# Loading the first chunk's alpha, k and q by batch instead of by pairs of batches, in a new instruction order

## The chip, the core and the metric

The kernel runs on one core of one Trainium2 chip. The core has five engines, each with its own queue of instructions that it executes in order: PE (TensorE, matrix products; its weight loads, PEld, overlap them), DVE (VectorE), ACT (ScalarE), POOL (GpSimd) and SP (SyncE, which in this kernel only issues transfers). Transfers (DMAs) run on 16 DMA engines beside them. A tile is a piece of the on-chip memory; a semaphore tells an engine that what it needs is ready. The metric is the device time of one execution in microseconds (us).

## What is computed

First a gated linear recurrence, for 4 batches of 8 heads with 768 tokens and 48 numbers per head. Then, with the heads side by side in rows of 384, a two-layer network with a norm before it and the rows added back behind it.

```python
def _attn_ref(q, k, v, alpha) -> np.ndarray:
    B, H, S, D = q.shape                      # 4, 8, 768, 48
    state = np.zeros((B, H, D, D), dtype=np.float32)
    y = np.zeros_like(q)
    for t in range(S):
        state = alpha[:, :, t, :, None] * state + np.einsum('bhd,bhe->bhde', k[:, :, t], v[:, :, t])
        y[:, :, t] = np.einsum('bhd,bhde->bhe', q[:, :, t], state)
    return y.astype(np.float32)

def _moe_ref(x, g_ln, w_ch1, w_ch2) -> np.ndarray:   # w_ch1 384 x 1536, w_ch2 1536 x 384
    mu = np.mean(x, axis=-1, keepdims=True)
    var = np.mean((x - mu) ** 2, axis=-1, keepdims=True)
    xn = (x - mu) / np.sqrt(var + 1e-06) * g_ln
    ch = np.maximum(xn @ w_ch1, 0.0) @ w_ch2
    return (x + ch).astype(np.float32)
```

The two weight matrices arrive as float64 and are rounded to float32 on the chip. q, k, v and alpha are float32 and lie in memory token by token, all heads of a token side by side.

## The kernel before

**Tiling.** The 768 tokens are cut into 6 chunks of 128. For each chunk c and batch b there is one unit of attention, 24 in all. Within a chunk the recurrence is written as matrix products. ACT takes the logarithm of alpha (L308), PE sums the logarithms over the tokens (L313), ACT takes the exponential of the sums and of their negatives (L320, L321), and DVE multiplies them with k (L323) and q (L325). PE transposes both products (L351), which are copied out of PE's accumulators by ACT and DVE (L356, L358). PE multiplies them to scores (chunk 0: L393), DVE keeps the causal part of these (L407, a predicated copy), and PE multiplies k with v to the chunk's contribution to the state (L428) and the scores, and the state before, with v and q to the output (L454 for chunk 0, L459 and L463 for the later ones).

**The gate.** A batch's new state is scaled by its decay over the chunk, which is the last row of the exponentials. This row has to become columns, so it goes through memory: SP sends the row out right behind the product with q (L330), and later fetches it back as columns (L419, the tile `gate`). In chunk 0 the DVE instruction that needs the gate is L437; later chunks add on DVE (L441) and scale on POOL (L443).

**The network.** The output of a batch is normed (L504 to L511) and transposed (L522). The first layer of chunk 0 is L558 (all four batches in two groups), its second layer L570. The network of chunks 1 to 5 is done later by a scheme that trades products for sums: combinations of weights and rows on DVE, ACT and POOL, then products (L848 for the first layer, L674 for the second), and sums of these into the result (L661, L684, L687, L690).

**Weights.** There are 12 pieces. Each is loaded as float64 words by SP (L203) and rounded by DVE and ACT (L215 to L232). The L558 of chunk 0 needs the first pieces.

**Loads.** `load(c, m, names)` loads what `names` lists of chunk c for the pair m of batches (2m and 2m+1): one transfer of 384 KB each for alpha, k and q, and v (L141). Chunk 0's alpha is the exception, loaded by batch (192 KB). All input loads, rows, gates and weights go through SP's one queue, in the order in which the program issues them.

**The order.** The program is written as generators, one for each unit of work, and each `yield` ends a step. The string ORDER holds one letter for each step: the step's instructions are put on the engines' queues when its letter comes. So ORDER decides what each engine does in which order, and nothing is reordered afterwards.

- `a` to `x`: the attention of unit n (a is chunk 0's batch 0, b its batch 1, e chunk 1's batch 0)
- `A` to `L`: load and rounding of a piece of weights
- `Y`, `Z`, `P`, `Q`: first and second layer of chunk 0
- `S`, `W`, `X`, `N`: combinations of weights and rows; `1`, `2`, `R`, `U`: hidden products and what follows them; `M`: products of the second layer; `O`: fetches rows kept in memory

```python
    with tc.manual_schedule():
        for turn in ORDER:
            next(turns[turn], None)
```

**At the start** the four alpha loads of chunk 0 are issued by the program before the ORDER loop begins. In the attention of chunk 0 the even batch (b = 0 and b = 2) has two steps ahead of its logarithm: one that loads k and q of its pair of batches, and one that loads v of the pair. The odd batch has none. After its row has been sent out (L330), the step that follows in the odd batch of chunks 0 and 1 loads alpha, k and q of the next chunk for the pair. In the trace batch 1's row of chunk 0 is sent out after batch 0's.

Of the kernel before, what the change touches and what calls it, by code (L numbers as in the profile page):

```python
# [11 lines left out]
FP32 = mybir.dt.float32  # L12
# [18 lines left out]


ORDER = (
    "bacabcadaacbcaadbcadabcababbebaccbadbaaBbccaedcbceAeeaaacbfecfBcdafddeaedbdeafae"
    "bcdccbfgadhAdcgCcdbebeebfhggdfgbfffbCdcgfgecdfchgdfhgabcddchdhAiiegjhacehedhhjfg"
    "biAdfidAeBhBijffYYiCjZZYYifZYlZCgjYDlYYjjZZYBZYgDieEgDgDjZZekEhZYGZgZigZGeeYgYgg"
    "fZYEhfGfkChihiYFYijfgEhgkhFZYhgYfghijgkFeZZlGZShfZYHlhHfYFYZeZHelYiZgllPmZkJIgJk"
    "PeiYjJIflHeSZIQgkIlYSjiPkffennSQlOKjLSnSjmSQhKnSjLnKPkiljnhSQnLkkjkWknkShOmPhkhl"
    "kOOhWlmmphmQmkmXjWQnXjlSQjPmkilXSXkP2OXWjXQjkjW2iXoSWX2oWX22Pi2mnol1j1mom2omSpoo"
    "l1XSpk2oW2m112p1m2pm11m1W211pp12O122r22jnn21lpnmnjSml1riOn2l12Rl111kqS1m21W1Rkp2"  # L40
    "o21mUXpq1mU2rUrnmj1rl2Rno2oomqonrormpokO1rNM2Mipin1op1ionoqUM2qp2W12RkMmNqiMoRtk"
    "UrpkqNM1NoMliMlNUMMNMNMKNqMlNorMWrnmtltNRMsqppMWNMriMMMpNlsqqqnoqttNttMtMsXMMssM"
    "sMNMNMX1oXXppMvstM2MXMMNMsppXoMXoqMsMMXM1nqqv11Xq1trMq2tqX21rn12v1r2ur2r222rvsqs"
    "svsu1rs1nuvvt2s11ss11p22rtsvosn2uropuXru222221uts212stnU1211u1121222Op1Rp2tRU21R"
    "Us1pXqU11x2tO2MM1vwMUM12xuRvu1vurNNNNwtOuuMwRxvNtxRNutwwMM2MOwNXwMNuXMMtNM1rMMMw"
    "qtXMMMxNUNxtMMsNMMMxXxMtXtrMMqMNrMXNvutMMwNuMMMNMMMxMLMOM11vvuq2X2O2wMus1wX11222"
    "2r2Xt1222w22utsqxvw2x2ww1vx21sX12121xwvq2O2x2w111u1uvU121w12s1wuRvx12U11J1q21R1U"
    "OvRxU121wMMu2xxsRNMw2NNMRM1MUNN2MMuUMqXN1MrNNRMNvMXNXMMMM2MMMxNM1uNXMMNMNMOXMXMv"
    "MMXOMMMXxNxwxMMvNMMMMMXMx21w1x222212v12w222x122w2212X11UX2212121121121wx111MU11X"
    "2RR2v1211212211R1URU211XOUM2XNRX1MX1RM2MXN2MXNXNMXXMXMMMN111U1MN1M1122MNM1MM2MM1"  # L50
    "11NNN121O11NM1MM21N1112N1122M1MMM12MM12N222M22M2RM1M2N22MM2MU1ON2M22M2UURR22RNNM"
    "MNM1MMOMRMNMUUM2ONMNNNMO2MMMUMNMMMMMRMMNNMMMNMNMMNMMMMMMMMNMNMMMMMMM"
)


# [1 line left out]
def kernel(  # L57
# [36 lines left out]
    nc = tc.nc  # L94

    B, S, H, D = q.shape
    DM = H * D
    DF = w_ch1.shape[1]
    P = 128
    NCB = S // P  # L100
    NP = H // 2
# [7 lines left out]
    raw = ctx.enter_context(tc.tile_pool(name="raw", bufs=B // 2))  # L109
# [10 lines left out]
    r = np.arange(P)  # L120
# [3 lines left out]
    raws = {}  # L124

    def load(c, m, names):

        bs = range(2 * m, 2 * m + 2)
        rows = slice(c * P, (c + 1) * P)
        for n, src in (("a", alpha), ("k", k), ("q", q)):  # L130
            if n in names:
                t = raw.tile([P, 2, 2, NP, D], FP32, name=f"r{n}", tag="in", bufs=7)
                step = 1 if n == "a" and c == 0 else 2
                for i in range(0, 2, step):
                    nc.sync.dma_start(
                        t[:, i:i + step].rearrange("t b i p d -> t b (i p d)"),
                        src[bs.start + i:bs.start + i + step, rows].rearrange("b t h d -> t b (h d)"))
                raws.update({(n, c, b): t[:, b - bs.start] for b in bs})
        if "v" in names:
            vn = raw.tile([P, 2, 2, NP, D], FP32, name="vn", tag="vn")  # L140
            nc.sync.dma_start(vn.rearrange("t b i p d -> t b (i p d)"),  # L141
                              v[bs.start:bs.stop, rows].rearrange("b t h d -> t b (h d)"))
            vx = None
            if c:


                vx = raw.tile([P, 2, NP, D], FP32, name="vx", tag="vx")
                src = v[bs.start:bs.stop, rows].rearrange("b (s t) h d -> s t b (h d)", s=2)
                parts = ((0, 0, NP, NP), (1, 0, NP, 0))
                if c >= SPLIT:  # L150
                    parts = ((0, 0, NP, NP - 1), (1, 0, NP - 1, 0), (1, NP - 1, 1, H - 1))
                for h, to, n, at in parts:
                    nc.sync.dma_start(
                        vx[halves[h]].rearrange("t b p d -> t b (p d)")[:, :, to * D:(to + n) * D],
                        src[1 - h, :, :, at * D:(at + n) * D])
            for b in bs:
                raws["v", c, b] = vn[:, b - bs.start], vx[:, b - bs.start] if c else None

    lone = {}

    def load_one(n):
# [11 lines left out]
    nc.scalar.dma_start(consts, nc.inline_tensor(const_np, name="consts").ap())  # L173
    tri, ident = consts[:, :P], consts[:, P:2 * P]
    mask, mask_of_halves = tri.bitcast(INT32), consts[:, 2 * P:].bitcast(INT32)
    for m in range(B // 2):
        load(0, m, "a")

    w1 = cpool.tile([P, NJ // 2, NF, 2 * P], FP32, name="w1")
    w2 = cpool.tile([P, NJ, DM], FP32, name="w2")  # L180
# [113 lines left out]
    def attention(c, b):  # L294


        whole, last = c == 0, c + 1 == NCB
        split = c >= SPLIT
        if whole and b % 2 == 0:
            load(0, b // 2, "kq")  # L300
            yield
            load(0, b // 2, "v")
            yield

        qk = qk_of(c, b).rearrange("t n p i c -> t n i p c")[:, :, :, :, :D]
        eq = eq_of(c, b).rearrange("t p i c -> t i p c")[:, :, :, :D]
# [143 lines left out]
        for p in range(NP):  # L450
            for i in range(2):
                for s in range(2):
# [5 lines left out]
                    r = i if split and p == NP - 1 else 1 - i  # L458
# [11 lines left out]
        if split:  # L470


            xv, m = x.rearrange("t (i p d) -> t i p d", i=2, d=D), NP - 1
# [446 lines left out]
    turns = {"YZ"[h]: first_of_chunk_0(h) for h in range(2)}  # L920
    turns |= {"PQ"[h]: second_of_chunk_0(h) for h in range(2)}
    turns |= {chr(ord("a") + n): attention(n // B, n % B) for n in range(NCB * B)}
    turns |= {chr(ord("A") + i): take_weights(i) for i in range(len(pieces))}
    turns |= {"M": mlp(), "S": combine_first(), "W": combine_weights(),
# [35 lines left out]
```

## Time and profile before

| | |
|---|---|
| median of 3 runs | 421.02 us |
| lowest and highest | 420.24 and 422.59 us |
| the profiled execution | 420.14 us |
| its span, first to last instruction | 418.3 us |
| PE busy | 409.8 us (98%), 4608 matmuls |
| DVE busy | 351.4 us (84%), 713 instructions |
| ACT busy | 177.5 us (42%), 440 |
| POOL busy | 151.6 us (36%), 164 |
| moved by DMA | 61.26 MB, 146 GB/s on the mean |

Busy times are those of one profiled execution, as shares of its span. An engine counts as busy while it executes an instruction; PE's matmuls overlap each other, so its busy time is no sum of pure work. The view by stage gives the same for stretches of the span. The chain of waits starts at the last instruction and goes back, at each step to what released it, so that it names the work that set the end. "issue" in it is time in which the engine waited for nothing that the profile shows, and "st L441" the tile and line of an instruction. Queue waits are those of SP: "SPq L419" is the place in SP's queue of the gate's transfer, with the time at which it was issued and how long the queue stood there. A landing is the time at which a transfer's last byte has arrived.

### The profile page before, as it was taken

To read this page: it belongs to the slowest core of one execution; us is meant where nothing else is said; L and a number is where in the kernel's file an instruction comes from. 1 tells how busy PE (TensorE), PEld (TensorE's weight loads), DVE (VectorE), ACT (ScalarE), POOL (GpSimd) and SP (SyncE) were. 2 spreads that over 40 slices of the span, in tenths; PEclk is the share of its full clock that TensorE was granted. 3 is DMA by queue.
4 is the path that set the end of the run, shared out by engine and by line. 5 is a ranking of instruction groups with operands and counts; after the bars stand their busy time and mean duration, and the time that the engine had idled before them with its cause. 6 is when DMAs were issued, how large, how long until landed. Compare 5 with 4: busy or idle time off the path is not lost.

```text
span 418.3 us, 11560 instructions
## 1 busy us (share of the span) xinstructions
PE 409.8 (98%) x4608; PEld 361.3 (86%) x4608; DVE 351.4 (84%) x713; ACT 177.5 (42%) x440; POOL 151.6 (36%) x164
## 2 busy tenths in 40 slices
PE   7998999999999999999999999999999999999996
PEld 5787888766578889998889999889998899999996
DVE  4999999999999989996888995688876767977873
ACT  5598447724243496414546603364313242014110
POOL 1011000003203980043395033493152940499123
PEclk9999999999999999999999999999999999999999
DMA  8999999987888778587684546433035200001201
GB/s 278 340 302 288 235 196 306 270 184 195 193 233 175 207 153 193 123 203 179 135 213 85 130 102 162 88 96 78 0 116 102 67 0 2 1 19 40 94 20 56
DMA packets 135037, 61.26 MB, mean 146 GB/s; under 512 B 90908, under 2 KB 131100, under 8 KB 134984
## 3 DMA queue, kind: packets, MB, share of 16 engines
q1 hardware_dynamic: 134440, 60.37, 56.1%
q8 instruction: 36, 0.59, 0.6%
q10 hardware_dynamic: 544, 0.17, 0.2%
q14 instruction: 17, 0.14, 0.1%
HBM read 43.12 MB, written 17.39 MB: 145 GB/s over the span
## 4 chain that ended last, share of the span: by engine, by line
PE 89%; DVE 4%; DMA 2%; ACT 2%; issue 1%; POOL 0%; POOLq 0%; SPq 0%; DVEq 0%
PE hps L848 31%; PE ops L674 30%; PE ops L570 8%; PE hps L558 7%; PE aps L401 3%; PE yps L459 2%; PE yps L463 2%; PE sums L428 2%; DMA vn<-in_v_dram 2%; PE xps L522 1%; PE aps L393 1%; DMA ra<-in_alpha_dram 1%; PE lps L313 1%; DVE w L217 1%; PE tps L351 1%
## 5 line engine op out<-in xcount | busy, mean ns | idle before, releaser
L690 POOL TENSOR_TENSOR ob<-ob,u 128x192 f32<-128x192 f32 x40 | 26.2, 665 | 64.5 <-DVE ob L687 48.3
L848 PE MATMUL hps<-sum,w 128*128 128x256 f32 x192 | 46.3, 381 | 0.0
L898 ACT ACTIVATE hT<-hT 128x512 f32<-128x512 f32 x48 | 28.7, 622 | 35.0 <-POOL hT L870 18.5
L443 POOL TENSOR_TENSOR mid<-mid,gate 112x192 f32<-112x192 f32 x20 | 11.6, 580 | 81.8 <-DVE mid L441 51.3
L674 PE MATMUL ops<-w,hT 128*128 128x192 f32 x224 | 40.5, 327 | 0.0
L848 PEld LDWEIGHTS hps<-sum,w 128*128 128x128 f32 x192 | 36.1, 190 | 5.0
L674 PEld LDWEIGHTS ops<-w,hT 128*128 128x128 f32 x224 | 37.1, 190 | 0.7 <-issue 0.2
L848 PE MATMUL hps<-xT,w 128*128 128x256 f32 x136 | 34.0, 380 | 0.0
L570 PE MATMUL ops<-w,hT 128*128 128x384 f32 x96 | 33.0, 492 | 0.0
L558 PE MATMUL hps<-xT,w 128*128 128x256 f32 x144 | 32.5, 382 | 0.0
L558 PEld LDWEIGHTS hps<-xT,w 128*128 128x128 f32 x144 | 27.0, 190 | 4.2
L674 PE MATMUL ops<-ws,sum 128*128 128x192 f32 x160 | 28.7, 327 | 0.0
L848 PEld LDWEIGHTS hps<-xT,w 128*128 128x128 f32 x136 | 25.5, 190 | 3.1
L570 PEld LDWEIGHTS ops<-w,hT 128*128 128x128 f32 x96 | 17.5, 190 | 10.8 <-DVE w L232 0.4
L674 PEld LDWEIGHTS ops<-ws,sum 128*128 128x128 f32 x160 | 26.5, 190 | 0.3
L684 DVE TENSOR_TENSOR ob<-ops,ob 128x192 f32<-128x192 f32 x50 | 17.2, 351 | 10.6 <-PE ops L674 6.5
L443 POOL TENSOR_TENSOR st<-st,gate 112x192 f32<-112x192 f32 x16 | 11.6, 725 | 35.6 <-DVE st L441 25.9
L674 PE MATMUL ops<-ws,hT 128*128 128x192 f32 x128 | 23.6, 328 | 0.0
L459 PEld LDWEIGHTS yps<-st,qT 48*64 48x64 f32 x320 | 19.9, 134 | 4.0 <-issue 2.3
L463 PE MATMUL yps<-vx,at 64*64 64x48 f32 x320 | 22.7, 219 | 0.0
L401 PEld LDWEIGHTS aps<-qT,kT 48*64 48x64 f32 x576 | 19.1, 134 | 4.1 <-issue 0.8
L459 PE MATMUL yps<-st,qT 48*64 48x48 f32 x320 | 22.0, 220 | 0.6 <-ACT x L486 0.6
(248 smaller groups left out, 1131.6 us busy)
## 6 DMA issues: line engine op xcount, KB each, us to landing
ws<-in_moe_w_ch_dram SPq DMA_DIRECT2D x12, 768.0 KB, 5.8
td<-tr SPq DMA_DIRECT2D x64, 96.0 KB, 2.8
vn<-in_v_dram SPq DMA_DIRECT2D x12, 384.0 KB, 6.9
kept<-x SPq DMA_DIRECT2D x24, 192.0 KB, 3.0
ob<-kept SPq DMA_DIRECT2D x24, 192.0 KB, 3.0
out_dram<-ob SPq DMA_DIRECT2D x19, 192.0 KB, 1.9
ra<-in_alpha_dram SPq DMA_DIRECT2D x16, 192.0 KB, 2.6
kT<-td SPq DMA_DIRECT2D x32, 96.0 KB, 3.4
```

The source lines that it names most:

```text
L401: nc.tensor.matmul(to, kT[rs, p, s], qT[rs, p, s], start=True, stop=True)
L428: nc.tensor.matmul(up[h, p], qk_of(c, b)[ts, 1, p, i, :h.stop - h.start], vn[ts, i, p], start=True, stop=True)
L443: nc.gpsimd.tensor_mul(new, new, by)
L459: nc.tensor.matmul(yps[i][halves[s], i, p], qT[rs, p, s], (now, mid)[s][rs, p], start=True, stop=r != i)
L463: nc.tensor.matmul(yps[r][halves[s], i, p], at[halves[r], p, s], by, start=r != i, stop=True)
L558: nc.tensor.matmul(hps, w1[:, j // 2, f, j % 2 * P:][:, :P], xT_of[0][:, f, bs], start=(f == 0), stop=(f == NF - 1))
L570: nc.tensor.matmul(ops_of[b], hT_of[c][:, j, b], w2[:, j], start=(j == 0), stop=(j == NJ - 1))
L674: nc.tensor.matmul(acc, lhs[:, j], rhs[:, j], start=(j == 0), stop=(j == NT - 1))
L684: nc.vector.tensor_add(x, acc, x)
L690: getattr(nc.gpsimd, f"tensor_{op}")(x, x, y)
L848: nc.tensor.matmul(acc[:, i], w, b, start=True, stop=True)
L898: nc.scalar.activation(out=x, in_=x, func=AFT.Relu)
```

## The change

Chunk 0's alpha, k and q are no longer loaded before the loop (alpha) or by pairs of batches (k and q). A new function `load_first(n, b)` loads one of them for one batch, 192 KB; the pair of batches still shares one tile, each batch filling its half. Each of the four attention units of chunk 0 begins with three steps of its own, one each for alpha, k and q, and each step is a letter of ORDER. v of a pair is loaded in one further step of the even batch, as before. `load` no longer needs its exception for alpha. Instead of 4 alpha loads and 4 loads of k and q, SP issues 12, so 4 more in all. ORDER, now with ten letters more for these steps, is a new string throughout; its first lines are shown.

```diff
 ORDER = (
-    "bacabcadaacbcaadbcadabcababbebaccbadbaaBbccaedcbceAeeaaacbfecfBcdafddeaedbdeafae"
-    "bcdccbfgadhAdcgCcdbebeebfhggdfgbfffbCdcgfgecdfchgdfhgabcddchdhAiiegjhacehedhhjfg"
...
+    "babcbbdaaccdbadacabcabcabdbcaadbcdcaabcaccebdaccacbfbaadabaaeBfecbdecdadbeefdAae"
+    "adbfeebeBcdgfahdcedcaabgdCbgcbggebchbefAdffffcdfgcdcdbbCcddhhahdebhgghegecfdAhhi"
...
 )
...
         for n, src in (("a", alpha), ("k", k), ("q", q)):
             if n in names:
                 t = raw.tile([P, 2, 2, NP, D], FP32, name=f"r{n}", tag="in", bufs=7)
-                step = 1 if n == "a" and c == 0 else 2
-                for i in range(0, 2, step):
-                    nc.sync.dma_start(
-                        t[:, i:i + step].rearrange("t b i p d -> t b (i p d)"),
-                        src[bs.start + i:bs.start + i + step, rows].rearrange("b t h d -> t b (h d)"))
+                nc.sync.dma_start(t.rearrange("t b i p d -> t b (i p d)"),
+                                  src[bs.start:bs.stop, rows].rearrange("b t h d -> t b (h d)"))
                 raws.update({(n, c, b): t[:, b - bs.start] for b in bs})
...
+    pairs = {}
+
+    def load_first(n, b):
+
+        src, m = {"a": alpha, "k": k, "q": q}[n], b // 2
+        if (n, m) not in pairs:
+            pairs[n, m] = raw.tile([P, 2, 2, NP, D], FP32, name=f"r{n}", tag="in", bufs=7)
+        t = raws[n, 0, b] = pairs[n, m][:, b % 2]
+        nc.sync.dma_start(t.rearrange("t i p d -> t (i p d)"),
+                          src[b, :P].rearrange("t h d -> t (h d)"))
+
...
-    for m in range(B // 2):
-        load(0, m, "a")
...
         whole, last = c == 0, c + 1 == NCB
         split = c >= SPLIT
-        if whole and b % 2 == 0:
-            load(0, b // 2, "kq")
-            yield
-            load(0, b // 2, "v")
-            yield
+        if whole:
+            for n in "akq":
+                load_first(n, b)
+                yield
+            if b % 2 == 0:
+                load(0, b // 2, "v")
+                yield
```

In the order built from the new string, SP issues at the start alpha of batches 1 and 0, k of 1, alpha of 2, q of 1, alpha of 3, k and q of 0, k and q of 2, k of 3, v of batches 0 and 1, q of 3, v of batches 2 and 3; then batch 1's row, alpha, k and q of chunk 1 (first pair), the rows of batches 0 and 2, batch 0's gate, batch 3's row, and the first weights. Before it was alpha of 0 to 3, k and q of the first pair, k and q of the second, v of both pairs, the rows of batches 0 and 1, alpha, k and q of chunk 1 (first pair), batch 2's row, batch 0's gate and the first weights. With the lines of the changed kernel, which lie 6 to 8 further down, L164 is the new load, L445 the old L437, L427 the gate's transfer and L566 the old L558.

More of the change, by code (lines that the diff above doesn't have):

```diff
@@ L33 @@
 ORDER = (
-    "bacabcadaacbcaadbcadabcababbebaccbadbaaBbccaedcbceAeeaaacbfecfBcdafddeaedbdeafae"
-    "bcdccbfgadhAdcgCcdbebeebfhggdfgbfffbCdcgfgecdfchgdfhgabcddchdhAiiegjhacehedhhjfg"
[L36 to L51, printed above, removed]
@@ L52 @@
-    "MNM1MMOMRMNMUUM2ONMNNNMO2MMMUMNMMMMMRMMNNMMMNMNMMNMMMMMMMMNMNMMMMMMM"
+    "babcbbdaaccdbadacabcabcabdbcaadbcdcaabcaccebdaccacbfbaadabaaeBfecbdecdadbeefdAae"
+    "adbfeebeBcdgfahdcedcaabgdCbgcbggebchbefAdffffcdfgcdcdbbCcddhhahdebhgghegecfdAhhi"
+    "feagddigjhAcAiiiBlfgBhjjYfiYYZBijYCjZeZkjfkYCDYDfigZYYZZYjDDZgZeYfYEeYgEhYjCZggh"
+    "higjleZEGfgFYYfGhYhYggEfZGZZZhiijfZYYFliZihkGhFYSkZFZjHiilHZhZYZlYifllgflHggHYPf"
+    "YeegIkJSOgIfnSZgJZlkkegPSkhnfeIQISZfjJKQKjleSQhhlKSmjhkOnSnhinmLeQjjPeLPnnjLSWkk"
@@ new lines @@
+    "kkOnPOmkWlhShkkhWlmQpmSmmkjXXmQPnmSXSQiXjXjikWXPW2XWQ122KiSW1Solojl1j2XPk2mWWk2l"
+    "m1Xomonm1ooo2op21jkp2pm2j1nW2pp1j1lm1212X11pi2mm222nSmnlm2r1l1nnS2q12q1Ulj221p12"
+    "1lkpo2rnR1jmOX1OWn1U1nRpk2iprir2O2RornoUoro1pkiooqrrM1ooM1p2NiOqkoRMom1NUMmq2mmk"
+    "pUqqMnR1NNtmMklMpMMWqNiol1lNMiMlNoMrMMpWtl2MlMMRNqMmmUsrNrpnNMopqotMXsNqsqqMnttt"
+    "qvtrtXnNMsMMMpMNpsMsq2uMNtMMNXsNqXMXuMXMsMMpMXM1oMMqsv1121qrtq22MXrrnortn2vX211v"
+    "1211222qqv1rrssssvsrXsqpvvxs2122st2u2t21s1uOso11pu11p2uUoX1ut21stp2w2n1212rO1112"
@@ new lines @@
+    "uR122Uv1p1nRtURsMNM2MqMp221twU21u21RtuOXNurtXruNRUuvOwNwvMMxrsrXutMxMMvNMMxXMtsR"
+    "uwN1NxMtMwwNsUNMxrsMMwMMMMxxNNtsNMJtNuv2MMMNMXXMNtMrMMMNMMXMMMqMuwvMMXuXXx222212"
+    "21vw1s1w22t2w21122xw2xvuX1O11wwM12v2xvv222s212212111xw2qx1212UO1U1x1R2R1w1Ut111R"
+    "1RwuMM1UOqrMuxR2NxN1MxtMUN2MqMvMNNuMMNMwMXrMNwwwN2w1MwM1qMONMUMvMNRNMMxXXNvMNMMM"
+    "vxMMXuNXxMNMMXMMMMMNMXv2wMMXMxv221212X22211v122M221111u12w1XO12Ox2x12222X111xU11"
+    "2UR1222O2URx22111Uu21R11X122u12NXUXX1MMXMNMXRLMRMX1NO212MXMUMNX12X211N1111RMM122"
@@ L53 @@
+    "M111MN12NNM11MM2M12R2MMX1NMN1M11M1211111NRN21222M2N1MRMNM2ONMMMMN2U22MMMM2R22O22"
+    "2MMM2M1U21MUN2OMNRMMUMNMNUMNMMMMMM2NONNNRUNNMMMNMMMMMMMMMMNMNMNMNMMMMMMMMMMMMM"
 )
```

## The prediction, written before the changed kernel was run

> **What bounds the kernel now.** I read the busy time by stage first, then the chain of waits, then the instructions in order of time on VectorE (DVE), ScalarE (ACT) and SyncE (SP) in the first 40 us, then the waits of SP's queue and of the gate tile.
>
> ```profile
> 10.00:20.00 10.00, 10.00 (x146) 7.76 (x145) 9.26 (x17) 5.06 (x12) 0.00 (x0) 1.00 1.05 340
> 20.00:30.00 10.00, 9.73 (x238) 8.82 (x237) 9.86 (x19) 9.43 (x31) 1.90 (x2) 1.00 1.05 320
> 30.00:40.00 10.00, 8.31 (x170) 6.92 (x171) 9.90 (x22) 8.68 (x22) 1.69 (x3) 1.00 0.92 278
> 40.00:125.00 85.00, 84.33 (x1123) 64.03 (x1122) 83.03 (x150) 40.57 (x97) 10.53 (x13) 1.00 0.89 227
> 300.00:400.00 100.00, 100.00 (x541) 94.01 (x540) 75.71 (x145) 24.03 (x48) 50.58 (x48) 1.00 0.17 46
> ```
>
> The columns are the stretch and then the busy time (and count) of PE, PE's weight loads, DVE, ACT and POOL, the granted clock, the DMA engines' share and GB/s. From 10 to 125 us DVE is full (29.0 of 30 us, then 83.0 of 85); from 300 on it has a quarter to spare and PE is full. "Busy" flatters PE early, since matmuls overlap; the chain shows who waits:
>
> ```profile
> 18.30 0.59 issue
> 18.89 0.71 DVE at L407
> 19.60 0.45 DVE w L215
> ...
> 35.45 0.28 DVE st L441
> 35.73 0.04 issue
> 35.77 0.52 PE sums L428 x26
> ...
> 313.08 24.17 PE hps L848 x112
> ```
>
> Between 18 and 36 us it is one DVE instruction behind the other; after that it is PE. The last line gives a pure PE step: 24.17 / 112 = 216 ns. Adding such steps for all 4608 matmuls (L674 163 ns, L570 323 ns, transposes 109 ns, the small attention matmuls 15 to 56 ns) gives 396.6 us of PE work. PE's clock position runs behind this sum by 11.7 us at 41 us, 14.2 at 120 us, 16.2 at 180 and 18.4 at the end, so a change can only act on those 18.4 us, and the early ones are DVE's.
>
> **The order built.** The instruction orders of both programs (no time in them) show that the reordering moves nothing across one mark: before the first L558 (38.76 us) PE has the same 23.2 us of real work in both, and the L229 that this L558 waits for has the same 52 DVE instructions before it, 28.3 us by their steps. So I follow DVE to that mark.
>
> **The start.** Batch 1 is worked on first in both. Before, ACT takes a second and a third logarithm before its first exponential:
>
> ```profile
> 4.51 0.94 ACT L308 ACTIVATE la<-ra 128x384 f32<-128x384 f32 x2 [2.49 <-DMA ra<-in_alpha_dram]
> 6.12 0.52 ACT L308 ACTIVATE la<-ra 128x384 f32<-128x384 f32 x1 [0.67 <-DMA ra<-in_alpha_dram]
> 6.73 0.49 ACT L320 ACTIVATE eq<-lps 128x384 f32<-128x384 f32 x1
> ```
>
> Afterwards its alpha is the first transfer (landing mark 3.72 us, not 4.48), and the exponential is third in ACT's queue. PE's warm-up matmuls end near 4.7; with 0.5 for L313 the exponential runs at 5.3, its inverse to 6.1, and DVE's first product starts at about 6.1, not 7.63: 1.5 us earlier. Batch loads in themselves free little: DVE waited for q for 0.28 us and never for k. The next products then wait for their own transfers: 1536 KB landed by 8.44 us, and the same bytes carry alpha, k and q of batches 0 and 1 afterwards. Counting steps (0.46 us a product, 0.60 a copy, 0.64 a predicated copy) with PE's transposes between them, DVE reaches its first L437 (the state times the gate, batch 0) at about 16.0. Before it got there at 17.64 with one L323 and one L325 more behind it, so at 16.71 for equal work. The gain is 0.7 us if nothing else stops it. The four extra DMA issues cost SP 4 x 0.45 = 1.8 us, which it spends while earlier transfers are in flight; SP's idle stretch from 10.84 to 12.61 covers it, and without it the loads behind would slip by as much.
>
> **The wait that is added.** That L437 needs the gate, which SP fetches from a row that another DMA has written:
>
> ```profile
> 7.25 1.42 SPq L330 DMA_DIRECT2D row<-eq  x2
> 8.71 0.40 SPq L135 DMA_DIRECT2D ra<-in_alpha_dram  x1
> 9.17 0.46 SPq L135 DMA_DIRECT2D rk<-in_k_dram  x1
> 9.67 0.46 SPq L135 DMA_DIRECT2D rq<-in_q_dram  x1
> 10.60 0.24 SPq L330 DMA_DIRECT2D row<-more  x1
> 12.61 0.37 SPq L419 DMA_DIRECT2D gate<-row  x1
> 13.03 0.50 SPq L203 DMA_DIRECT2D ws<-in_moe_w_ch_dram  x1
> ...
> SPq L419 <- DMA row<-eq: 1.7, 1, 1.7
> ```
>
> A 2 KB row issued at 7.25 held the gate until 12.61, because v, issued before it, landed only at 12.62: the row goes behind all bytes queued earlier. The next row, issued at 10.60 behind chunk 1's alpha, k and q, landed at 15.97, together with that q (15.98). In the new SP order batch 0's row stands behind those three loads (batch 1's turn, which issues them, comes first), and its gate is the next thing but one. Equal bytes are ahead, so the row lands at 16.0 and the gate is issued then. To its landing the gate tile's rows give
>
> ```profile
> DMA to landing us min/median/max: 2.7/3.0/3.4
> ```
>
> from issue; the queue is empty by then, so I take 2.6 (one gate at 56.63 landed at 59.14): 18.6. DVE, in order, stands from 16.0 to 18.6, and with it the L407, L323, L325 and first weight rounding queued behind. Against equal work at 16.71 that is **+1.9 us**. Behind the gate on SP stands the first weight load (13.03 before, 16.7 now); it needs 5.1 us (that view's shortest), lands at 21.8, and DVE comes to it at 18.6 + 3.8 = 22.4, so it is just hidden. The second gate lands behind those weights, at 21.9, and is wanted 3.0 us of DVE steps after the first, at 21.6: **+0.3** more. The lower bound is the case in which the row does not queue (rival 1), the upper each small load costing more (rival 3).
>
> **What becomes of it.** DVE waits 1.0 us in all between 40 and 125 us (0.4, 0.2, 0.2 and 0.2), so it can't make up the loss. For each matmul that waits for DVE I took DVE's steps up to what it waits for, less PE's steps up to it. Before, this lead that DVE must have peaks at 2.56 us (an L463 after 120.8 us of PE work; DVE's own position is 11.1 late there, and 11.1 + 2.56 is close to PE's 14.2). In the new order it peaks at 3.16 (an L428, a batch's state sums, after 110.8 us): **+0.6**. Other terms between stay under these peaks in both. At the end the new order takes two L661 additions (0.61 each on the chain) off the way of the last POOL group; PE's last matmul then decides, so **-0.3** of the 0.7 us that they delayed.
>
> Sum: 1.9 + 0.3 + 0.6 - 0.3 = **+2.5 us**. The profiled execution took 420.14 us (span 418.3, and 1.8 around it), so 422.6 in its terms; the median of the three runs is 421.02, 0.9 above it, so **423.5**.
>
> **Rivals.**
> 1. *No gate wait; the early start stays.* One place, the first L437: if the row lands by 13.4 (issue 10.4 and the 3.0 us that the very first load took), the gate is there at 16.0. Then -0.7 + 0.6 - 0.3 = -0.4: 420.6. For it: nothing but the chance that the row's engine runs ahead of the others; against it: three rows that each landed with the bulk before them. It decides where the row lands 2.6 us before the bulk ahead of it does. 13%.
> 2. *DVE is held, but PE does not feel it*, the lead being smaller in fact than the sums of steps say, since PE loses time of its own from 110 to 200 us (0.8 us at 114 on ACT's copy): half the loss, 422.3 or, with the lead's 0.6 gone too, 421.7. 15%.
> 3. *Small loads are slow.* The four alphas (192 KB) landed 0.79 us apart, the 384 KB ones 1.05. If the former is their cost, eight loads take 8 x 0.79 - 4 x 1.05 = 2.1 us more, and the row, the gate and the weights slip by as much: 425.6. Against it: between the alphas the constants (160 KB) and 384 four-byte elements of g were moved. 12%.
> 4. *The search paid off later*: the 6.7 us by which PE falls back after 41 us (18.4 less 11.7) halve and the start costs nothing: 421.0 - 3.3 = 417.7. No row speaks for it; the sums of steps after 125 us are alike. 10%.
>
> [...]
>
> **How the numbers follow.** The forecast has 50%, the rivals 13, 15, 12 and 10. Range 419.4 to 427.0: it takes in rivals 1 to 3 and late weights (about 1 us more), and leaves out 4 and a few per cent above; the forecast's own is 422.3 to 425. A measurement of this kernel can tell about 0.5% (2.1 us; the three runs spread over 2.4) from no change. Below 418.9: rival 4 and a little, 11%. Above 423.1: rival 3 and three quarters of the forecast, whose centre is 423.5 and whose spread is upward, 50%. The rest 39%.
>
> **What would show it.** In the new profile: first L323 near 6.1; SP's first gate issue near 16 with a wait for the row; a DVE gap of 2 to 2.6 us before the first L445 (the old L437), ended by the gate's DMA; the first L566 (old L558) 1 to 2 us after 38.76; last POOL group ending before the last matmul. It is wrong if that gap is under 1 us, or if the gap is there and the first L566 comes no later.

## The result, and the profile after

| | before | changed |
|---|---|---|
| median | 420.69 us (6 runs) | 427.64 us (6 runs) |
| lowest and highest | 420.12 and 422.59 | 426.28 and 429.21 |
| profiled execution, its span | 420.14, 418.3 | 427.81, 426.0 |

The ratio is 1.0161, with a 95% interval of 1.0134 to 1.0187: 5.6 to 7.9 us slower. The prediction was 423.5 us, at most 427.0. It had the right sign and named the main wait of the start, but it put only 0.6 us on all that follows the start, where about half of the loss lay.

The busy time by stage of the changed kernel, with the same stretches and columns as before (PE, PE's weight loads, DVE, ACT, POOL, granted clock, share of the DMA engines, GB/s):

```profile
10.00:20.00 10.00, 9.03 (x131) 7.25 (x129) 6.49 (x13) 5.12 (x13) 0.00 (x0) 1.00 0.66 210
20.00:30.00 10.00, 8.26 (x184) 7.34 (x184) 9.25 (x18) 6.39 (x21) 0.95 (x1) 1.00 1.00 325
30.00:40.00 10.00, 6.81 (x130) 5.62 (x128) 9.58 (x20) 7.99 (x25) 1.66 (x3) 1.00 1.00 285
40.00:125.00 85.00, 83.80 (x1146) 63.05 (x1144) 82.97 (x148) 39.46 (x94) 8.45 (x13) 1.00 0.92 230
300.00:400.00 100.00, 99.89 (x535) 92.94 (x534) 79.13 (x149) 30.25 (x65) 51.92 (x48) 1.00 0.18 49
```

DVE lost 2.8 us of busy time from 10 to 20 us (6.49 against 9.26), and there the DMA engines' share fell to 0.66 (1.05 before). From 40 us on, busy times hardly tell the two kernels apart. SP's queue from the first row to the first weights:

```profile
8.85 0.30 SPq L338 DMA_DIRECT2D row<-eq  x1
9.20 0.40 SPq L133 DMA_DIRECT2D ra<-in_alpha_dram  x1
9.64 0.53 SPq L133 DMA_DIRECT2D rk<-in_k_dram  x1
10.27 0.47 SPq L133 DMA_DIRECT2D rq<-in_q_dram  x1
10.81 0.55 SPq L338 DMA_DIRECT2D row<-eq  x1
12.25 0.24 SPq L338 DMA_DIRECT2D row<-more  x1
17.70 0.39 SPq L427 DMA_DIRECT2D gate<-row  x1
18.19 0.29 SPq L338 DMA_DIRECT2D row<-more  x1
18.53 0.40 SPq L209 DMA_DIRECT2D ws<-in_moe_w_ch_dram  x1
```

Batch 0's row went out at 10.81 us, behind chunk 1's three loads, and the gate 6.9 us later; the first weights follow at 18.53 (13.03 before). The chain of waits runs through just this:

```profile
10.81 6.87 DMA row<-eq
17.68 0.02 issue
17.70 2.09 DMA gate<-row
19.79 0.03 issue
```

In VectorE's instructions in order of time, the bracket gives the idle time before an instruction and what ended it:

```profile
15.65 1.36 DVE L415 COPY_PREDICATED at<-consts,aps 128x512 f32<-128x512 int32 x2
19.91 0.36 DVE L445 TENSOR_TENSOR st<-sums,gate 112x192 f32<-112x192 f32 x1 [2.90 <-DMA gate<-row]
...
23.71 0.36 DVE L445 TENSOR_TENSOR st<-sums,gate 112x192 f32<-112x192 f32 x1 [0.68 <-DMA gate<-row]
```

The two stands add to 3.6 us. The kernel before had none, as its instructions show:

```profile
17.64 0.35 DVE L437 TENSOR_TENSOR st<-sums,gate 112x192 f32<-112x192 f32 x1
...
21.54 0.35 DVE L437 TENSOR_TENSOR st<-sums,gate 112x192 f32<-112x192 f32 x1
```

The first L566 of PE starts at 42.6 us (38.76 before).

The measure that the prediction used, lateness, is the time at which an engine stands in its work less the sum of the steps that it has done. In us, worked out from the traces:

```
                          at 41 us       at 120   at 180    at the end
                        DVE     PE         PE       PE         PE
before                  9.75   11.69     14.17    16.16      18.39
changed                13.90   15.30     18.90    22.32      26.12
more                    4.15    3.61      4.73     6.16       7.73
```

So about half of it is lost in the first 41 us and half afterwards, most of that from 120 us on.

### The profile page after: what moved, and what is told of

The parts are those of the page before. It is cut to its first block, busy times and chain, and to the rows that moved or that the text cites. A ratio compares the mean times of both kernels' runs of the same rounds, so it can differ in the third digit from the quotient of the medians.

```text
span 426.0 us, 11574 instructions
## 1 busy us (share of the span) xinstructions
PE 411.6 (97%) x4608; PEld 361.0 (85%) x4608; DVE 354.0 (83%) x713; ACT 178.6 (42%) x440; POOL 152.0 (36%) x164
## 4 chain that ended last, share of the span: by engine, by line
PE 74%; DVE 14%; DMA 7%; ACT 2%; issue 1%; POOL 0%; SPq 0%; DVEq 0%; POOLq 0%
PE hps L856 31%; PE ops L682 30%; PE yps L467 3%; DMA rk<-in_k_dram 2%; PE yps L471 2%; DVE ws L231 2%; PE ops L578 2%; PE hps L566 2%; DMA ws<-in_moe_w_ch_dram 2%; PE aps L409 2%; DMA row<-eq 2%; DVE w L223 2%; DVE w L238 1%; PE sums L436 1%; DMA ra<-in_alpha_dram 1%
## 5 line engine op out<-in xcount | busy, mean ns | idle before, releaser
L566 PE MATMUL hps<-xT,w 128*128 128x256 f32 x144 | 32.6, 383 | 0.0
L566 PEld LDWEIGHTS hps<-xT,w 128*128 128x128 f32 x144 | 26.9, 190 | 3.7
L578 PEld LDWEIGHTS ops<-w,hT 128*128 128x128 f32 x96 | 17.7, 190 | 10.8
L471 PE MATMUL yps<-vn,at 64*64 64x48 f32 x320 | 22.3, 220 | 0.0
L682 PE MATMUL ops<-more,sum 128*128 128x192 f32 x120 | 22.0, 326 | 0.0
```

Source lines behind the costliest of these rows:

```text
L471: nc.tensor.matmul(yps[r][halves[s], i, p], at[halves[r], p, s], by, start=r != i, stop=True)
L566: nc.tensor.matmul(hps, w1[:, j // 2, f, j % 2 * P:][:, :P], xT_of[0][:, f, bs], start=(f == 0), stop=(f == NF - 1))
L578: nc.tensor.matmul(ops_of[b], hT_of[c][:, j, b], w2[:, j], start=(j == 0), stop=(j == NJ - 1))
L682: nc.tensor.matmul(acc, lhs[:, j], rhs[:, j], start=(j == 0), stop=(j == NT - 1))
```

## The experiments

A ratio is each time that of the kernel to the kernel before, run beside it on the same chip. 0.1% is 0.42 us. The kernel before ranged over 419.8 to 426.7 us in these runs, so that medians are less sharp than ratios.

### Start and rest exchanged

ORDER can be cut ahead of the first L558 (L566) step, at which both sequences have done almost the same work: the new start followed by the old rest, and the other way round. Each letter keeps its count, and what the start has done is left out of the rest.

```diff
- old start (pair loads), old rest
+ e1: old start (pair loads), new rest
- new start (batch loads), new rest
+ e2: new start (batch loads), old rest
```

> The kernel before up to its first L558 step (pair loads, old sequence), then the rest of the new sequence. The new start left VectorE 4.1 us later than the old one at 41 us (13.9 against 9.75) and the kernel 6.95 us slower. Theory A (the start carries all of it, the later 3 us follow from VectorE being late): 421.0 to 421.6 us, that is 420.7, 0.6 for the higher lead of VectorE that the new rest needs (3.16 against 2.56 us), and up to 0.6 at the seam. Rival B (the new rest loses about 3 us by itself, from 120 us on): 424 to 425 us.

Measured: 425.12 us, ratio 1.0071 (1.0024 to 1.0118).

> The changed kernel up to its first L566 step (batch loads, new sequence), then the rest of the old sequence. Theory A (a late VectorE costs more later on, whatever the rest is): about 427 us. Rival B (the start costs the 3.6 to 4.1 us that engines are late at 41 us, the rest of the 6.95 belongs to the new rest): 424.3 to 424.8 us.

Measured: 424.94 us, ratio 1.0071 (1.0043 to 1.0100).

Rival B holds in both, each time a little above its range: start and rest cost 3.0 us each (1.8 to 4.2 and 1.0 to 5.0), and their sum, 6.0, is near the 6.8 measured. Lateness passes through: from 41 us to the end PE fell back by another 10.8 us in the changed kernel, 11.0 in e1 and 10.5 in e3 (below), although these came to 41 us with 15.3, 12.4 and 12.4. The new rest takes its 11 us whatever the start does; the old one took 6.7 in the kernel before and 8.6 in e2, so there a part of what the start cost came up only later.

### The row's place

```diff
 order of steps in ORDER
-  batch 1: load chunk 1's alpha, k, q;  batch 2: exponentials;  batch 0: product with q, row out
+  batch 2: exponentials;  batch 0: product with q, row out;  batch 1: load chunk 1's alpha, k, q
```

> The changed kernel with one step moved: batch 1's step that loads chunk 1's alpha, k and q comes behind batch 0's row and not ahead of it. The row (issued at 10.81, landed at 17.68) should then land right behind v, at about 14.6 us, and the gate with the last of the three loads, at 17.7, not 19.8. VectorE's stand before the first L445 falls from 3.0 to about 0.8 us. If the start passes one to one to the end: 427.6 - 2.2 = 425.4 us; if lateness is multiplied (6.95 at the end for 4.15 at 41 us): 424 us. If the row's place is not what holds the gate, the stand stays near 3 us and the time at 427.6.

Measured: 424.62 us, ratio 1.0087 (1.0043 to 1.0130), so about 3.1 us less than the changed kernel (1.0161); the two intervals just clear each other. VectorE's instruction in this kernel:

```profile
18.24 0.36 DVE L445 TENSOR_TENSOR st<-sums,gate 112x192 f32<-112x192 f32 x1 [1.57 <-DMA gate<-row]
```

The gate was issued at 13.70 and came at 18.12. It still came behind chunk 1's loads, which end later here (17.30) than before (15.98). The shorter stand alone proves little, because stands differ between executions. e2 has the changed kernel's start, with the row behind the loads. Its first stand was no longer in its profiled execution, and both together were 2.6 us:

```profile
18.17 0.36 DVE L445 TENSOR_TENSOR st<-sums,gate 112x192 f32<-112x192 f32 x1 [1.53 <-DMA gate<-row]
...
22.31 0.36 DVE L445 TENSOR_TENSOR st<-sums,gate 112x192 f32<-112x192 f32 x1 [1.02 <-DMA gate<-row]
```

There batch 0's row, issued at 11.01, landed at 15.93, ahead of chunk 1's q (16.92). What the row's place costs has to be taken from the times.

The opposite was tried in the kernel before, with its loads and its sequence kept:

```diff
-        nc.sync.dma_start(row[:ne], eq_of(c, b)[ends].rearrange("o p i c -> o (p i c)"))
+        send_row = partial(nc.sync.dma_start, row[:ne],
+                           eq_of(c, b)[ends].rearrange("o p i c -> o (p i c)"))
+        if (c, b) == (0, 0):
+            late_rows.append(send_row)
+        else:
+            send_row()
...
             load(c + 1, b // 2, "akq")
+            while late_rows:
+                late_rows.pop()()
```

> The kernel before, its sequence and loads unchanged, with one edit: batch 0's row is sent out behind chunk 1's first alpha, k and q, as in the changed kernel, and no longer ahead of them. The row then lands with the last of these, at 16.0 us, and the gate behind it is issued at 16.0 and not 12.61. Theory (the row's place holds gate and first weights): the gate lands at 18.1 to 18.6 us, VectorE, ready at 17.6, stands 0.5 to 1 us, then as much again for the first weights, which are issued 3.5 us later; 1 to 2.5 us in all: 421.7 to 423.2 us. Rival (a late gate is taken up elsewhere): 421.2 us or less.

Measured: ratio 1.0057 (1.0024 to 1.0090), 2.4 us; median 423.79. VectorE's instructions in order of time:

```profile
18.67 0.36 DVE L445 TENSOR_TENSOR st<-sums,gate 112x192 f32<-112x192 f32 x1
19.12 1.34 DVE L415 COPY_PREDICATED at<-consts,aps 128x512 f32<-128x512 int32 x2
22.07 0.56 DVE L216 TENSOR_SCALAR w<-ws 128x768 int32<-128x768 int32 x1 [1.61 <-DMA ws<-in_moe_w_ch_dram]
```

With pair loads VectorE is busy until the gate is there, and hardly stands for it (0.4 us in the first 40). It stands 1.6 us for the first weights, whose transfer SP issued at 16.09 and not 13.03, because the waiting gate was in front. The row's place costs about 2.4 us (1.0 to 3.8) even where VectorE hardly stands for the gate.

### Small loads, or few places in flight

First the rates that the DMA engines reached in the kernel before, then in the changed one:

```profile
5.50:8.50 3.00, 1.61 (x5) 0.68 (x4) 0.59 (x2) 2.29 (x6) 0.00 (x0) 1.00 1.06 381
8.50:12.50 4.00, 4.00 (x38) 3.25 (x36) 3.94 (x8) 2.95 (x7) 0.00 (x0) 1.00 1.06 381
```

```profile
5.50:8.50 3.00, 1.42 (x4) 0.30 (x2) 0.56 (x1) 2.32 (x6) 0.00 (x0) 1.00 1.04 376
8.50:12.50 4.00, 3.75 (x26) 2.82 (x26) 3.49 (x7) 3.34 (x8) 0.00 (x0) 1.00 0.89 270
```

From 5.5 to 8.5 us queued loads of 192 KB ran at 376 GB/s (381 before; six of them landed 0.51 us apart, from 7.44 to 9.97), then the engines ran dry (270). SP's waits up to 19 us in the changed kernel say why:

```profile
SPq L427 <- DMA row<-eq: 4.3, 1, 4.3
SPq L164 <- DMA ra<-in_alpha_dram: 1.2, 3, 0.6
...
SPq L164 <- DMA rk<-in_k_dram: 0.7, 1, 0.7
```

Issues of loads wait for other loads that they don't need. In the traces of both kernels the transfers report their landings to eight semaphores in turn, and each of the ninth to the sixteenth was issued only after the transfer eight places earlier had landed: in the changed kernel batch 2's k is issued at 5.52, when batch 1's k has landed (5.50); batch 3's k at 6.93, when batch 2's alpha has (6.91). Eight loads of 384 KB hold twice the bytes of eight of 192 KB. Three kernels test this.

```diff
 e4, changed kernel:
             for n in "akq":
-                load_first(n, b)
+                if n == "a":
+                    load_first(n, b)
+                elif (n, 0, b) not in raws:
+                    load(0, b // 2, n)
                 yield
 e7, kernel before (load_first as in the change):
-            load(0, b // 2, "kq")
+            for i in ((b + 1, b) if b == 0 else (b, b + 1)):
+                for n in "kq":
+                    load_first(n, i)
 e8, kernel before:
+    tiny = [cpool.tile([1, 16], FP32, name=f"tiny{i}") for i in range(4)]
...
-            load(0, b // 2, "kq")
+            for n in "kq":
+                load(0, b // 2, n)
+                nc.sync.dma_start(tiny[b + (n == "q")], v[b, :1, 0, :16])
```

> The changed kernel with k and q of chunk 0 loaded by pairs of batches again (384 KB, 4 loads in place of 8; alpha stays by batch; the sequence is kept, the odd batch's steps for k and q are empty). In the changed kernel the DMA engines moved 76 to 110 KB per half microsecond from 8.5 to 12.5 us, against 130 before, while SP's loads waited for loads issued eight transfers earlier. Theory (at most eight transfers are in flight, and smaller ones mean fewer bytes): the dry stretch goes, the last of chunk 1's loads lands at 16.0 and not 17.5, the gate follows 1.5 us earlier, and so does VectorE: 425 to 426 us. Rival (the row and the gate are late by their place in the queue alone): the stand before L445 keeps its 3.0 us, 427.6 us.

Measured: 426.41 us, ratio 1.0113 (1.0079 to 1.0146), 2.0 us less than the changed kernel, though the intervals overlap. The forecast's 76 to 110 KB and 130 KB per half microsecond are about the numbers of packets there; in KB it was 114 to 159 against 181 to 194. Chunk 1's last load landed at 16.63 (17.50 in the changed kernel). But VectorE came to the first L445 only at 18.65 (17.0), and stood 0.39 us there.

> The kernel before with its sequence unchanged, and one edit: k and q of chunk 0 by batch (8 loads of 192 KB in place of 4 of 384 KB, at the same two places). Theory (at most eight transfers in flight, so smaller ones hold fewer bytes): from 8 to 13 us the DMA engines move about 290 GB/s and not 381, the last of chunk 1's first loads lands near 17.3 and not 15.98, batch 0's gate about 1 us later: 421.2 to 422.5 us. Rival (k and q of the batch worked on first come earlier, and that is worth more): 420.3 us or less.

Measured: 422.20 us, ratio 1.0030 (0.9993 to 1.0067): likely slower, not clear of zero. Chunk 1's last load landed at 17.09 and batch 0's gate at 17.27 (16.17 before). That is late, but not by much: in the five profiled kernels that have the old loads of chunk 0 in their old order (the kernel before, e1, e9, e13, e14) that load landed at 15.98 to 16.95.

> The kernel before with its pair loads, and a load of 64 bytes behind each of the four loads of k and q of chunk 0; nothing reads them. This takes as many places in flight as the batch loads do, with large transfers and no more bytes. Theory (eight places in flight): a dry stretch as with the batch loads, SP's v loads and rows issued later, chunk 1's last load lands after 16.5 us, 421 to 422.5 us. Rival (it is the size of the transfers that costs): the DMA engines keep 380 GB/s between 8 and 13 us, that load lands near 16.0, 420.7 us.

Measured: 423.36 us, ratio 1.0041 (1.0019 to 1.0063). Chunk 1's last load landed at 18.05. The same stretch in e4, e7 and e8:

```profile
8.50:12.50 4.00, 4.00 (x14) 2.19 (x15) 2.58 (x5) 2.83 (x7) 0.00 (x0) 0.61 1.07 378
```

```profile
8.50:12.50 4.00, 3.61 (x25) 2.81 (x27) 3.68 (x8) 3.76 (x9) 0.00 (x0) 1.00 0.98 325
```

```profile
8.50:12.50 4.00, 3.81 (x28) 3.01 (x30) 3.68 (x8) 3.56 (x9) 0.00 (x0) 1.00 1.00 327
```

Pairs in the changed kernel bring 378 GB/s back. Four loads of 64 bytes in the kernel before bring the rate down as far (327) as eight loads of 192 KB in place of four of 384 do (325). Both lie below the 365 to 381 of the five kernels with the old loads. Here it is the places, not the size. Nor is it the time that SP takes for four more issues: in e8 its issues at 6.19, 6.98 and 7.96 follow landings at 6.18, 6.90 and 7.95.

### Why pairs did not bring the start back

Both faults of the new start undone (row ahead, k and q by pairs: the edits of e3 and e4), with the old rest; and the same start with batch loads:

> The changed kernel's start with both of its faults undone (batch 0's row ahead of chunk 1's loads, k and q of chunk 0 by pairs), then the rest of the old sequence. The start with the row ahead left VectorE at 10.8 us of lateness at 41 us, against 9.75 before; k and q by pairs should bring back half a microsecond to one. Theory (the 6.95 us are the start's row and loads, and the new rest): 420.5 to 422 us, no slower than 0.3% above the kernel before. Rival (something else in the new start costs time): 423 us or more.

Measured: 422.27 us, ratio 1.0035 (0.9999 to 1.0072).

> The changed kernel's start, with its batch loads and with batch 0's row ahead of chunk 1's loads, then the rest of the old sequence. What is left of the change is the batch loads and the new sequence before the first L566. They left VectorE at 10.8 us of lateness at 41 us, against 9.75 in the kernel before, and the loads alone cost 0.3% in the old sequence. Theory (row and rest are the two large parts): 421.2 to 422.5 us, that is 0 to 0.4% above the kernel before. Rival (a new start of this kind costs 3 us whatever the row does): 424 us or more.

Measured: 422.95 us, ratio 1.0041 (1.0012 to 1.0070); that is 1.3 us less than e2, whose row is behind the loads, and not clear of zero.

Without the row's place and the new rest, 0.4% is left of 1.6%. The row ahead does not rule the stand out: in the profiled execution of e12 the gate was issued at 14.21 and landed at 19.81, and VectorE stood 3.1 us before L445, twice as long as in e3. What differs between e6 and e12 is within the intervals, though the DMA engines moved 379 GB/s from 8 to 13 us with pairs (e6) and 291 with batch loads (e12). In e4 the granted clock (third number from the end) was 0.61 where it is 1.00 in the kernel before. In e6 it was 0.5 for 3.41 us:

```profile
6.78:10.20 3.42, 1.54 (x5) 0.49 (x4) 1.58 (x4) 2.29 (x6) 0.00 (x0) 1.00 1.07 389
10.20:13.61 3.41, 3.41 (x13) 2.69 (x13) 2.13 (x4) 1.75 (x5) 0.00 (x0) 0.50 1.07 375
```

One such stretch takes 0.4% off the mean clock of an execution (half of 3.41 us in the 421.4 of e6's span; its clock was 0.996). The ten executions of e6 divide by it: five with a mean clock of 1.000 took 421.2 to 422.0 us, five with 0.992 to 0.996 took 422.5 to 427.4 (median of the kernel before beside them: 421.16). So pairs and row together bring the start back to within about 1 us where the clock holds. This division was made afterwards, not set up as an experiment. An attempt to start VectorE earlier met the same thing:

```diff
-    for m in range(B // 2):
-        load(0, m, "a")
...
+    for b in (1, 0, 3):
+        load_alpha(b)
...
         if whole and b % 2 == 0:
+            if b:
+                load_alpha(b)
             load(0, b // 2, "kq")
```

In ORDER, batch 2's logarithm and batch 1's exponential change places.

> The kernel before with its pair loads and its sequence, and two edits at the start: alpha of batches 1, 0 and 3 first, then k and q of the first pair, then alpha of batch 2 (before: alpha of 0, 1, 2, 3 ahead of them), and batch 2's logarithm behind batch 1's exponential. No more transfers than before, each as large. If VectorE sets the time from its first product on: that product starts 0.7 us earlier (6.9 and not 7.6 us), v, rows and gates land as before, and the time is 0.4 to 0.7 us less than the kernel before, 420.0 to 420.3 us. If a gate or a row decides instead: no difference.

Measured: 424.81 us, ratio 1.0103 (1.0072 to 1.0134): a clear miss. Alpha of batch 3 landed at 6.31 (6.09 before, as the fourth). Its logarithm stands ahead of the first exponential on ScalarE, so that VectorE's first product came at 8.21 and not at 6.9. PE was out of work from 7.3 to 10.0 us, and its clock was 0.5 from 10.43 to 13.84. e11 gives it work there:

```diff
             nc.tensor.matmul(lps[:, :DM], tri, las.pop((c, b)), start=True, stop=True)
+            if b == 0:
+                more_idle = ps.tile([P, 512], FP32, name="lps", tag="bank", bufs=6)
+                for _ in range(6):
+                    nc.tensor.matmul(more_idle[:, :P], zero, zero, start=True, stop=True)
```

> The kernel with the other alpha order (424.8 us), and six more matmuls on zeros (2.6 us of TensorE's time) behind batch 0's running sums; nothing reads them. There TensorE stood from 7.3 to 10.0 us, and its granted clock was 0.50 from 11 to 13 us, in the transposes that VectorE waits for (as in the two kernels with k and q by pairs, whose clock fell to 0.5 between 9 and 13 us). Theory (the clock falls because TensorE idles, and that costs VectorE its start): the clock stays at 1.00, VectorE's lateness at 41 us falls from 13.4 to about 11.2, and the time to 422 to 423 us. Rival (the clock has nothing to do with it, alpha of batch 2 comes too late): 424.5 us or more.

Measured: 425.03 us, ratio 1.0067 (1.0029 to 1.0104), so the gain is not clear of noise, and smaller than forecast. The stretch itself, first in e10, then in e11:

```profile
10.00:14.00 4.00, 3.99 (x13) 2.83 (x14) 0.96 (x2) 2.27 (x5) 0.00 (x0) 0.57 1.07 374
```

```profile
10.00:14.00 4.00, 4.00 (x32) 3.19 (x34) 2.48 (x5) 2.66 (x6) 0.00 (x0) 1.00 1.07 375
```

With the extra products the clock stays at 1.00, PE does 32 matmuls in place of 13 (six of them at most the extra ones), and VectorE's lateness at 41 us is 11.65 in place of 13.49. The profiled execution of e11 lost this again: its clock fell from 73.03 to 76.45 us, and VectorE's wait of 2.8 us for ScalarE, which waited for PE, ended at 77.46.

```profile
69.61:73.03 3.42, 1.36 (x65) 1.28 (x66) 3.08 (x7) 1.85 (x7) 0.00 (x0) 1.00 1.00 313
73.03:76.45 3.42, 3.11 (x9) 2.47 (x9) 1.56 (x3) 0.00 (x0) 0.00 (x0) 0.50 0.99 375
```

This execution took 427.34 us. The ten executions of e11 divide as those of e6 do: five with a mean clock of 0.999 or 1.000 took 422.2 to 424.0 us, five with 0.995 or 0.996 took 426.0 to 427.3. In e10 all six were at 0.991 to 0.996.

### The rest

In the new rest PE stood at three places for a ScalarE instruction that empties the accumulator bank that PE needs next. From three views of PE in e3, in order of time:

```profile
121.86 1.13 PE L856 MATMUL hps<-xT,extra 128*128 128x256 f32 x4 [0.68 <-ACT hT L886]
...
139.37 0.25 PE L467 MATMUL yps<-st,qT 48*64 48x48 f32 x1 [0.28 <-ACT x L494]
...
163.33 0.92 PE L682 MATMUL ops<-w,hT 128*128 128x192 f32 x4 [0.45 <-ACT xT L532]
```

```diff
 order of steps in ORDER, added to e3
-  second-layer products (P), ..., hidden product (2), ..., hidden product (1)
+  ..., hidden product (2), ..., second-layer products (P), hidden product (1)
-  outputs of unit l, copy of unit m, ..., hidden product (1)
+  copy of unit m, ..., hidden product (1), outputs of unit l
-  logarithm of unit t, norm of unit m, ..., copy of unit k (L532)
+  copy of unit k (L532), logarithm of unit t, norm of unit m, ...
```

> The kernel with the row ahead (424.6 us), and five letters moved at three places of the new rest, where TensorE stood until ScalarE had copied out the accumulator bank it had just filled: 0.84 us at 121.9 (L856 behind L886's copy), 0.46 at 139.4 (L467 behind L494) and 0.61 at 163.3 (L682 behind L532). A group of second-layer products goes between the two at the first place, a hidden product at the second, and at the third ScalarE's copy goes ahead of a logarithm and a norm. Theory (these waits belong to the new rest, and nothing behind them would have stopped TensorE anyway): 1.9 us less, 422.7 us, and TensorE's lateness grows between 120 and 180 us by 1.7 and not 3.6. Rival (TensorE stops a little later for VectorE or the transfers all the same): 424 us or more.

Measured: 426.49 us, ratio 1.0127 (1.0073 to 1.0180): the rival. Two of its four executions had a mean clock of 0.992 and 0.995 (427.9 and 428.6 us); the two at 1.000 took 424.1 and 425.1, as e3 did. PE fell back 3.95 us between 120 and 180 us, no less than in e3 (3.64). PE in e5, where it stood a little later:

```profile
153.37 0.24 PE L409 MATMUL aps<-qT,kT 48*64 48x64 f32 x1 [1.18 <-DMA gate<-row]
```

The program makes this L409 wait for two transfers, the transposed k and q of its batch read back from memory. e3 has no such wait of PE there. So one wait took the place of others: taking PE's waits away one by one did not pay.

The rest was cut once more, at 165 us of PE's work (about 180 us of the span):

```diff
- old start, old middle, old end
+ e9:  old start, old middle, new end
+ e14: old start, new middle, old end
```

> The kernel before up to 165 us of TensorE's work (about 180 us of the span), then the rest of the new sequence. The old start with all of the new rest was 3.0 us slower than the kernel before. Of what TensorE lost there beyond the old sequence, 2.1 us lay between 120 and 180 us, where its waits follow VectorE and transfers closely, and 1.4 us after 180, where VectorE has slack. If the middle carries most of it: 421.5 to 422.3 us here. If the end carries it all: 423.7 us.

Measured: 422.77 us, ratio 1.0041 (1.0018 to 1.0065).

> The kernel before up to its first L558 step, then the new sequence up to 165 us of TensorE's work, then the old sequence to the end. The new rest cost 3.0 us (1.0 to 5.0), its end alone 1.7 (0.8 to 2.7). If the two parts add up: 1.3 us here, 421.5 to 422.5 us. If the middle costs nothing by itself and the new end costs more behind the new middle: 421.1 us or less. If the middle costs all of it and the end was an effect of its seam: 423.5 us.

Measured: 424.32 us, ratio 1.0095 (1.0057 to 1.0134).

The end costs 0.8 to 2.7 us, the middle 2.4 to 5.6, both together 1.0 to 5.0 (e1). Both count; the middle likely has more. Its 4.0 us are above all three forecasts, and 1.7 and 4.0 do not add up to e1's 3.0, though the intervals allow it. The 4.0 include a wait of PE for VectorE of 0.83 us at 210.8 us, behind the seam, which neither sequence has. What holds the new rest back stays open beyond e5.

## Why the prediction went wrong, point by point

- **VectorE's earlier start.** Its first product came at 6.29 us (6.1 forecast). But the second waited 1.74 us for batch 0's k, and VectorE reached the first L445 at 17.0, not 16.0. Of the 0.7 us of gain nothing was left (equal work before: 16.71).
- **The row behind chunk 1's loads.** Right, and the main wait of the start. The row landed at 17.68 and not at 16.0, the gate 2.09 us after its issue and not 2.6, so the first stand was 2.90 us and its end 1.2 us later than forecast. The second was 0.68 us (0.3 forecast). The rule behind it, that a row lands behind all bytes queued earlier, holds only roughly: in e2 and e13 the row landed 1.0 and 0.7 us before chunk 1's last load. The 2.6 us by which rival 1 had it ahead were not seen.
- **"The four extra DMA issues cost SP 1.8 us ... SP's idle stretch covers it."** This step failed. I counted SP's time and missed what an issue waits for. With smaller loads in the same eight places the engines ran dry, and chunk 1's last load landed at 17.5 and not 15.98. Rival 3 put 2.1 us on the small loads; alone (e7) they cost 1.3 us, not clear of zero, and by another mechanism. Its slow small loads are not there: queued ones landed 0.51 us apart, not 0.79. The size of the loads thus does not explain the loss: queued 192 KB loads ran at 376 GB/s, and from 8.5 to 12.5 us the rate fell as far with k and q by pairs in e8 (327 GB/s) as with k and q by batch in e7 (325).
- **The size of the start.** 1.9 + 0.3 us were forecast. At 41 us PE was 3.6 us later in the profiled execution, and e2 measured 3.0 (1.8 to 4.2).
- **"Other terms between stay under these peaks in both", +0.6 us for the whole rest.** This step failed too, and it cost most: e1 measured 3.0 us (1.0 to 5.0). I had followed one kind of wait, PE on VectorE, in a sequence that was new throughout. Waits of PE on ScalarE's copies and on transfers were left out, and so was VectorE waiting for PE: from 120 to 180 us PE fell back 3.4 us (2.0 before), from 180 us to the end 3.8 (2.2 before). Which of these waits carries the 3.0 us stays open: three of them were moved in e5, and nothing was gained.
- **The end.** The last POOL group ends at 422.48, ahead of the last matmul's end at 422.88, as forecast.
- **A row misread.** "Batch 1 is worked on first in both" is wrong for the kernel before: only its logarithm is. The exponentials and products of batch 0 come first there. The sum did not rest on it.

## What to carry to other kernels

A transfer's place in its queue can cost more than its bytes: a 2 KB row sent out behind 1.1 MB cost 2.4 us here (1.0 to 3.8, e13), and as its reader sat in the same queue, the next weights were late too (issued at 16.09 and not 13.03). Smaller loads came earlier here only at first: batch 1's k landed at 5.50 and not 7.41, but with eight places in flight the rate then fell to 270 GB/s (381 before), and chunk 1's last load landed at 17.50 and not 15.98. Compare bytes in flight, and not only issue times. And where a sequence is new throughout, the start that one understands is not the change: cut the two sequences at a point of equal work and exchange the halves.

## What the runs showed of the hardware

Four loads of 64 bytes in a queue of large ones brought the rate from 8.5 to 12.5 us down to 327 GB/s (e8), against 365 to 381 in the five profiled kernels with the old loads. Each took one of eight places, and the large loads behind were issued only as earlier ones landed (6.19 us behind a landing at 6.18, 6.98 behind 6.90).

TensorE's granted clock was 0.5 from 10.43 to 13.84 us in e10. In the 3.42 us before that, as long a stretch, TensorE was busy for 0.68 us (longest gap 2.74). In e11, with six useless products more, the longest gap there was 2.44 us, and the clock stayed at 1.00 from 8 to 14 us. e4, e6 and e11 (from 73.03 us) show the same 3.41 to 3.42 us at 0.5, after 3.42 us with 1.63, 1.54 and 1.36 us of work. A limit can't be read from this: e11 had 1.61 us of work from 8.18 to 11.59 us and kept its clock. What sets the clock is not shown here.
